# Three of 56 zero-fill pieces leave the Pool queue in parts of 4, 105, 13 and 6 rows

## The chip, the cores and the metric

The kernel runs on one core of one Trainium2 chip. A core has five instruction streams that matter here: TensorE (PE, with its weight loads as PEld), VectorE (DVE), ScalarE (ACT), GpSimd (POOL) and SyncE (SP), and sixteen DMA engines that move data between HBM and the on-chip memory. The metric is the device time of one execution in microseconds, and less is better. Times of whole runs are medians; durations inside a run come from one profiled execution.

## The reference

The reference computes a forward pass and its gradient for one token through four residual layers: attention (A), feed-forward (B), and the same A and B once more with the same weights.

```python
def _A_ref(x, k_cache, v_cache, wq, wo):
    W = min(4096, max(256, Sk // 4))                # 4096 of 32768 positions
    q = (x @ wq).reshape(B, Sq, Hq, Dh)             # 32 heads of 128
    k = jnp.repeat(k_cache[:, :, Sk - W:, :], rep, axis=1)
    v = jnp.repeat(v_cache[:, :, Sk - W:, :], rep, axis=1)
    p = softmax(q @ k * Dh ** -0.5)
    return (p @ v) @ wo
def _B_ref(x, w1, b1, w2):
    h = x @ w1 + b1
    return (h * tanh(softplus(h))) @ w2
x = x + _A_ref(_layernorm(x), ...); x = x + _B_ref(_layernorm(x), ...)   # twice
```

The outputs are x, and the gradients with respect to x, the two caches, wq, wo, w1, b1 and w2. The attention sees only the last 4096 of 32768 positions of each cache, so seven eighths of the two cache gradients, 56 MiB of bf16, are zeros and still have to be written.

## The kernel before, in words

All matrices are streamed from HBM in chunks of 128 rows by 4096 bf16 values (1 MiB, 8 KiB a row) through a ring of eight slots plus a few borrowed homes (`Ring`, issues at line 71 on the SP queue). A slot that is released lets the next load in the list start. The forward pass multiplies chunk by chunk, the backward pass turns chunks with TensorE (line 474) or takes row dots on VectorE (line 451). At the end the weight gradients are formed as outer products in PSUM (`unit_dw`, line 1051; `units_kv`, line 1086), copied out by `evac` to VectorE (line 306) or ScalarE (line 309), whichever a running cost count has as less loaded, and stored by `store` (lines 1025 and 1030) on the SP queue, in transfers of 512 KiB to 1 MiB. Before those outer products can start, row forms of the vectors are gathered with small transfers: `rowize` (line 1015), `rowize_f` (line 861), `take_back` (line 819) and `twins` (line 1043), all of them on SP.

The schedule is written by hand: each engine runs its instructions in program order, and the framework adds semaphore waits. Transfers of one queue take their completion semaphores from eight in turn, so an issue waits until the transfer that used that semaphore before is complete.

The zeros are 56 pieces of 128 rows by 4096 values. The list `zjobs` holds their destinations, `zt` is an on-chip tile of zeros, and `zeros(n, after)` issues the next n pieces on the Pool queue (line 265). With `after`, Pool first copies one element of a tile that the computation is about to write (line 260, into `pz`), so that the pieces are held back until that value exists. Calls of `zeros` are spread over the program from the second forward layer on. The ones of the last attention backward layer (`attn_bwd(0, ...)`) sit in its hooks: 2 pieces in `do1` at chunk 5, 4 in `dp1`, 4 in `dq1` once `DQC` is there, 2, 1 and 1 in `dn1` at t = 3, 6 and 7, and 2 after the layer. Counted from 0, `dq1` issues pieces 46 to 49.

Other instructions on Pool at that time are the copy at line 909 (before `dp1`'s pieces) and the one-element copies. On SP the loads are over by then; the small transfers of the list above and later the stores stand in its queue.

Of the kernel before, what the change touches and what calls it, by code (L numbers as in the profile page):

```python
# [15 lines left out]
P = 128  # L16
# [77 lines left out]
def kernel(  # L94
# [22 lines left out]
    nc = tc.nc  # L117
# [13 lines left out]
    def sb(shape, dtype, name):  # L131
        return keep.tile(shape, dtype, name=name)
# [24 lines left out]
    ZC = 4096  # L157
    zt = sb([P, ZC], BF16, "zt")
# [36 lines left out]
    for hi in range(4):  # L195
        r = slice(32 * hi, 32 * hi + 32)
# [9 lines left out]
    DQC = sb([P, HQ, 2], BF16, "DQC")  # L206
# [39 lines left out]
    zjobs = []  # L246
    for out_t in (out_2, out_3):
        for g in range(G):
            dst = out_t[0, g, 0:ZR, :].rearrange("(p r) d -> p (r d)", p=P).rearrange("p (r c) -> p r c", c=ZC)
# [7 lines left out]
    def zeros(n, after=None):  # L257

        if after is not None and zjobs:
            nc.gpsimd.tensor_copy(pz[0:1, pz_n[0] % 16:pz_n[0] % 16 + 1], after[0:1, 0:1])  # L260
            pz_n[0] += 1
        for _ in range(n):
            if zjobs:
                dst = zjobs.pop()
                nc.gpsimd.dma_start(dst, zt[:])  # L265


    KEEP_Q = (5, 6, 7)
# [519 lines left out]
    def last_da(k):  # L788

        for c in (5, 6):  # L790
            if k == 0:
                da_dots(c)
            else:
                ring.release(("2", 0, c))
        if k:
            nc.gpsimd.memset(zt[:], 0.0)
            zeros(1)

    def wo_hook1(c):
        if c == 0:  # L800
            zeros(7, OC[:, 0, 1:2])
        if c:
            conv(1)
# [18 lines left out]
    put_by("OC", OC, HQ)  # L822
    put_by("NA", NA, TD)
    zeros(8, x3)
    sB1 = mlp_fwd(1, x3, st3, lambda: conv(1, "A"))
    put_by("NB", NB, TD)
# [180 lines left out]
    def rowize(cols, n, base, off):  # L1007

        b = big().bitcast(BF16)
        nc.tensor.transpose(b[0:2 * n, 0:P], cols[:].rearrange("p n l -> p (n l)"), ident_bf[:])  # L1010
        k = rt_n[0]
        rt_n[0] += 1
        nc.scalar.copy(rt[0:2 * n, k, :], b[0:2 * n, 0:P])
        for l in range(2):
            nc.sync.dma_start(ROWS[base + l:base + l + 1, off:off + n * P].rearrange("o (t p) -> o t p", p=P),
                              rt[l:2 * n:2, k, :])
# [40 lines left out]
    def units_rows(base, nblk, out):  # L1057

        for c in range(nblk // 4):
            s = stage_free.popleft()  # L1060
            for tt in range(4):
                n = 0
                while n < 2:
                    m = unit_dw(base, NOFF + (4 * c + tt) * P, 512 * n, s[:, tt * D + n * 512:(tt + 1) * D], 2 - n)
                    n += m
                    store(out.rearrange("(c p k) d -> p c (k d)", p=P, k=4)[:, c], s, 2 * tt + n - m, 2 * tt + n, 8,
                          c == nblk // 4 - 1)
                    yield
# [110 lines left out]
    def dq1():  # L1179
        stage_free.extendleft(KT[:, g].rearrange("p t d -> p (t d)") for g in range(G))  # L1180
        todo[1].append(units_rows(32, HQ, out_5))
        rowize(DQC, HQ, 0, NOFF)
        zeros(4, DQC[:, 0, 0:1])

    def dn1(t):
        if t in (3, 6, 7):
# [8 lines left out]
    def units_a0(k):  # L1195
# [3 lines left out]
        work(4)  # L1199

    g0 = attn_bwd(0, sA0, g1, ("o", 3), ("q", 3), (), dict(do=do1, dp=dp1, dq=dq1, dn=dn1), units_a0)
    zeros(2, g0)
    g0b = sb([P, TD], BF16, "g0b")
# [49 lines left out]
```

## Time and profile before

| | |
|---|---|
| median of three timed runs | 450.8 us (450.39 to 451.2) |
| profiled execution | 450.36 us |
| its span | 448.6 us |
| bytes moved, mean rate | 181.40 MB, 404 GB/s |
| HBM read, written | 81.84 MB, 98.62 MB |
| zero pieces on queue 0 | 56 issues of 1024 KB, 20.5 us from issue to landing (median) |
| first and last issue of a zero piece | 114.7 and 334.7 us |
| queue 8 (instructions) | 44 packets of 16 KB |

The page's line of engines gives busy time, share of the span and number of instructions. The slices cut the span in 40 equal parts. In the table of stretches a line has the stretch, its length, the busy time of PE, PEld, DVE, ACT and POOL with their instruction counts, the granted TensorE clock, the busy share of the 16 DMA engines and the GB/s moved. The share is a sum of packet times over 16 engines and can pass 1 by a per cent, since the packets of an engine overlap a little. A wait line reads: engine, what it was about to do, what it waited for, microseconds in total, times, longest. A timeline line has start, length, engine, line and operation, how often, and in brackets the idle time before it with what ended it. Beside these views the trace has the time of each completion increment: a transfer over 16 engines has 16 of them.

### The profile page before, as it was taken

How to read it: one execution, taken by the hardware profiler on the slowest of the kernel's cores; microseconds unless marked ns; L12 is line 12 of the kernel's file. 1: busy time of each engine (PE TensorE's matmuls, PEld its weight loads, DVE VectorE, ACT ScalarE, POOL GpSimd, SP SyncE). 2: the span in 40 equal slices, each digit the busy share in tenths (PEclk: the TensorE clock that was granted, in tenths of full speed). 3: DMA queues.
4: the chain of work that ended last, by engine and by line, in shares of the span. 5: the costliest groups of instructions: out<-in, count | busy, mean ns of one | idle time of the engine just before them, and what ended most of it. 6: DMA issues, size and time to landing. Idle time of an engine off the chain costs nothing.

```text
span 448.6 us, 12825 instructions
## 1 busy us (share of the span) xinstructions
PE 313.9 (70%) x5681; PEld 239.7 (53%) x5681; DVE 261.2 (58%) x516; ACT 210.0 (47%) x242; POOL 38.9 (9%) x86
## 2 busy tenths in 40 slices
PE   3845542465699797986988666797966988899600
PEld 3735532455586686986986545787941222235300
DVE  4504746367551664864477447663566999998600
ACT  2501101011058576870474441570647999999600
POOL 1000000001222212102101001012130000000000
PEclk9955555556559899995798657986765555555555
DMA  8999999979999999999999999999999999999993
GB/s 336 420 420 418 421 420 418 418 312 427 393 421 422 422 420 415 398 420 423 424 423 422 427 423 419 424 393 422 424 406 415 400 417 419 417 421 408 377 408 143
DMA packets 28085, 181.40 MB, mean 404 GB/s; under 512 B 3674, under 2 KB 3702, under 8 KB 9590
## 3 DMA queue, kind: packets, MB, share of 16 engines
q1 hardware_dynamic: 19874, 121.84, 66.1%
q0 software_dynamic: 8064, 58.72, 31.5%
q8 instruction: 44, 0.72, 0.6%
q14 instruction: 11, 0.09, 0.1%
q10 hardware_dynamic: 92, 0.02, 0.0%
HBM read 81.84 MB, written 98.62 MB: 402 GB/s over the span
## 4 chain that ended last, share of the span: by engine, by line
DMA 53%; PE 22%; ACT 7%; DVE 7%; issue 4%; SPq 1%; ACTq 0%; DVEq 0%
DMA ring<-in_B_w_dram 13%; DMA W<-in_A_wo_dram 8%; PE BIG L474 8%; DMA ring<-in_A_wq_dram 7%; DMA ring<-in_A_wo_dram 5%; DMA W<-in_A_wq_dram 5%; ACT ring L309 4%; DMA out_dram<-W 4%; DMA W<-in_B_w_dram 4%; PE TP L493 3%; DMA W<-dr_AC 2%; DMA W<-in_A_k_cache_dram 2%; PE wide L1051 2%; DVE KT L306 2%; PE SC L347 2%
## 5 line engine op out<-in xcount | busy, mean ns | idle before, releaser
L309 ACT COPY ring<-BIG 128x1024 bf16<-128x1024 bf16 x52 | 51.5, 1014 | 49.3 <-PE BIG L474 45.0
L1051 PE MATMUL wide<-W 2*128 2x512 bf16 x232 | 51.7, 597 | 10.7 <-ACT ring L309 1.7
L474 PE MATMUL BIG<-ident_bf,ring 128*128 128x128 bf16 x672 | 54.3, 233 | 1.8 <-issue 1.0
L474 PEld LDWEIGHTS <-ring 128*128 128x128 bf16 x768 | 52.0, 108 | 3.4 <-issue 2.6
L451 DVE CUSTOM_DVE_ANT_0 junk<-ring,SC 128x1024 bf16<-128x1024 bf16 x32 | 38.9, 1215 | 11.6 <-DMA ring<-in_B_w_dram 11.2
L1051 PEld LDWEIGHTS <-W 2*128 2x128 bf16 x240 | 12.6, 102 | 48.1 <-issue 43.7
L493 PEld LDWEIGHTS <-ring 128*128 128x128 bf16 x864 | 29.9, 98 | 10.0 <-issue 5.8
L309 ACT CAST ring<-wide 128x1024 bf16<-128x1024 f32 x35 | 33.9, 1040 | 2.0 <-PE wide L1051 0.9
L265 POOL DMA_DIRECT2D out_dram<-zt x56 | 29.7, 534 | 50.3 <-DMA out_dram<-zt 49.3
L306 DVE CAST ring<-wide 128x1024 bf16<-128x1024 f32 (+1 forms) x29 | 32.3, 1145 | 2.5 <-PE wide L1102 1.2
L309 ACT COPY KT<-BIG 128x1024 bf16<-128x1024 bf16 x22 | 21.6, 1007 | 21.4 <-PE BIG L652 19.5
L451 DVE CUSTOM_DVE_ANT_0 junk<-ring,DSX 128x1024 bf16<-128x1024 bf16 x24 | 29.4, 1224 | 0.8
L306 DVE COPY ring<-BIG 128x1024 bf16<-128x1024 bf16 x32 | 21.8, 689 | 12.8 <-PE BIG L474 10.2
L474 PE MATMUL BIG<-ident_bf,W 128*128 128x128 bf16 x280 | 23.8, 235 | 3.4 <-DMA W<-in_A_wo_dram 2.5
L309 ACT COPY W<-BIG 128x1024 bf16<-128x1024 bf16 x20 | 20.0, 1015 | 10.0 <-PE BIG L474 9.8
L536 PE MATMUL MV<-NA,ring 128*128 128x1 bf16 x512 | 15.3, 165 | 13.2 <-DMA ring<-in_A_wq_dram 11.7
L536 PEld LDWEIGHTS <-ring 128*128 128x128 bf16 x512 | 14.7, 104 | 14.0 <-DMA ring<-in_A_wq_dram 12.5
L474 PEld LDWEIGHTS <-W 128*128 128x128 bf16 x288 | 19.3, 115 | 4.0 <-DMA W<-in_A_wo_dram 2.6
L1102 PE MATMUL wide<-W 32*128 32x256 bf16 x128 | 20.0, 403 | 0.9 <-ACT ring L309 0.6
L347 PE MATMUL YR<-ring,AC 128*32 128x256 bf16 x208 | 11.1, 372 | 11.7 <-DMA ring<-in_B_w_dram 9.3
L309 ACT CAST KT<-wide 128x1024 bf16<-128x1024 f32 x18 | 17.7, 1064 | 3.2 <-PE wide L1051 3.0
L306 DVE CAST KT<-wide 128x1024 bf16<-128x1024 f32 (+1 forms) x14 | 15.4, 1141 | 6.3 <-PE wide L1051 6.2
(272 smaller groups left out, 521.3 us busy)
## 6 DMA issues: line engine op xcount, KB each, us to landing
out_dram<-zt POOLq DMA_DIRECT2D x56, 1024.0 KB, 20.5
ring<-in_A_wq_dram SPq DMA_DIRECT2D x24, 1024.0 KB
ring<-in_A_wo_dram SPq DMA_DIRECT2D x14, 1024.0 KB
ring<-in_B_w_dram SPq DMA_DIRECT2D x13, 1024.0 KB
W<-in_A_wo_dram SPq DMA_DIRECT2D x10, 1024.0 KB
W<-in_B_w_dram SPq DMA_DIRECT2D x8, 896.0 KB
out_dram<-ring SPq DMA_DIRECT2D x13, 512.0 KB
out_dram<-ring SPq DMA_DIRECT2D x6, 1024.0 KB
```

Of the source, the lines that this page charges most:

```text
L265: nc.gpsimd.dma_start(dst, zt[:])
L306: nc.vector.tensor_copy(dst, src)
L309: nc.scalar.copy(dst, src)
L347: nc.tensor.matmul(bank[32 * j:32 * j + 32, 0:n].rearrange("p (g a) -> p g a", a=m.shape[-1]), lhsT=vec.to_broadcast([P, 32]), rhs=m, star ...
L451: nc.vector.tensor_tensor_reduce(out=out, in0=a, in1=vec, scale=1.0, scalar=acc if i else 0.0, op0=ALU.mult, op1=ALU.add, accum_out=acc)
L474: nc.tensor.transpose(b[:, i * P:(i + 1) * P], block(w, i) if block else w[:, i * P:(i + 1) * P], ident_bf[:])
L493: nc.tensor.matmul(out, lhsT=w[:, i * P:(i + 1) * P], rhs=rhs_of(i), start=fresh[0], stop=last and i == n - 1, skip_group_check=True)
L536: nc.tensor.matmul(q_ps[:, h:h + 1], lhsT=ch[:, h * P:(h + 1) * P], rhs=NA[:, t, l:l + 1], start=(k == 0 and h == 0), stop=(k == TD - 1), ...
L1051: nc.tensor.matmul(b[:, 512 * i:512 * i + 512], lhsT=R[at:at + 2, lo:lo + P], rhs=R[at:at + 2, ro + 512 * i:ro + 512 * i + 512], start=Tru ...
L1102: nc.tensor.matmul(b[:, k * 256:(k + 1) * 256], lhsT=RT[32 * g:32 * g + 32, a, tp, :], rhs=YS[32 * g:32 * g + 32, :], start=True, stop=Tru ...
```

## The change

In `dq1` the call for four pieces is replaced by one whole piece and three that are cut into parts. The new function `zeros_beside` issues, for each piece, three transfers of 4, 105 and 13 whole rows, and one for the last 6 rows in which the 8 KiB rows are seen as 16 blocks of 512 bytes, with the block index outermost on both sides. The bytes written are the same, and so is their source, a tile of zeros.

```diff
+    SPARED = 3
+
+    def zeros_beside(n):
+        for _ in range(n):
+            dst = zjobs.pop()
+            at = 0
+            for k in (SPARED + 1, 105, 16 - SPARED):
+                nc.gpsimd.dma_start(dst[at:at + k, :], zt[at:at + k, :])
+                at += k
+            r = P - at
+            nc.gpsimd.dma_start(dst[at:P, :].rearrange("a (b c) -> b a c", b=16),
+                                zt[0:16, 0:r * (ZC // 16)].rearrange("b (a c) -> b a c", a=r))
...
     def dq1():
...
         rowize(DQC, HQ, 0, NOFF)
-        zeros(4, DQC[:, 0, 0:1])
+        zeros(1, DQC[:, 0, 0:1])
+        zeros_beside(3)
```

On the Pool queue the four issues of line 265 after the copy of `DQC` become one issue of line 265 and twelve in the order 4, 105, 13, 16x6 blocks, three times over (lines 277 and 280 of the changed kernel). Each of the thirteen takes the next of the eight semaphores. No other engine's instructions change or move.

## The prediction

> **What bounds the kernel now.** I read the page's slices first, then the DMA queues, then a table of stretches, then the tail by itself, then the Pool engine's instructions, then the waits.
>
> ```profile
> PE 313.9 (70%) x5681; PEld 239.7 (53%) x5681; DVE 261.2 (58%) x516; ACT 210.0 (47%) x242; POOL 38.9 (9%) x86
> ...
> GB/s 336 420 420 418 421 420 418 418 312 427 393 421 422 422 420 415 398 420 423 424 423 422 427 423 419 424 393 422 424 406 415 400 417 419 417 421 408 377 408 143
> ...
> q1 hardware_dynamic: 19874, 121.84, 66.1%
> q0 software_dynamic: 8064, 58.72, 31.5%
> q8 instruction: 44, 0.72, 0.6%
> ```
>
> No compute engine passes 70%, while the transfers run at about 420 GB/s in nearly every slice: the kernel is bound by its 16 DMA engines. Queue 1 carries loads and results (issued by SP), queue 0 the zero pieces (issued by Pool), queue 8 the fetching of instructions.
>
> ```profile
> 340.00:352.00 12.00, 10.23 (x44) 2.26 (x44) 11.83 (x11) 11.98 (x14) 0.00 (x0) 0.50 1.01 412
> 352.00:354.00 2.00, 1.48 (x11) 0.46 (x10) 2.00 (x3) 1.84 (x4) 0.00 (x0) 0.50 0.87 342
> 354.00:418.00 64.00, 57.73 (x314) 21.15 (x315) 58.50 (x56) 61.03 (x66) 0.00 (x0) 0.50 1.01 416
> 418.00:422.00 4.00, 3.79 (x26) 2.11 (x21) 3.62 (x4) 3.82 (x5) 0.00 (x0) 0.50 0.81 326
> 422.00:441.00 19.00, 0.00 (x0) 0.00 (x0) 1.06 (x1) 0.30 (x1) 0.00 (x0) 0.50 1.01 403
> 441.00:447.50 6.50, 0.00 (x0) 0.00 (x0) 0.00 (x0) 0.00 (x0) 0.00 (x0) 0.50 0.07 28
> ```
>
> The last two columns are the DMA engines' busy share and GB/s. Compute is over by about 423; the rest is draining stores. From 441.0 the share is 0.07, one sixteenth. Finer, in 40 slices of 437 to 449 us:
>
> ```profile
> GB/s 396 437 410 437 382 410 369 437 382 437 437 423 314 55 55 41 27 27 27 27 27 27 27 27 27 27 14 27 27 27 27 27 27 27 0 0 0 0 0 0
> ```
>
> 27 GB/s is a sixteenth of 437. **One DMA engine works alone for 6.3 us, from 441.0 to 447.3, and the kernel ends with it.** The span is 448.6, the profiled execution 450.36, the median of the three timed runs 450.8.
>
> How that engine came to be late stands in the trace's semaphore records: each transfer of 128 rows has 16 landings, one for each engine's 8 rows. Some zero pieces, numbered from 0 (us):
>
> ```
> piece  issued  1st landing  15th    16th
>   #9   142.14    158.14    160.71  160.80
>  #22   174.66    193.52    198.77  203.86
>  #42   304.24    309.43    312.27  315.63
>  #43   304.77    311.97    314.78  319.12
>  #44   305.29    314.39    317.24  321.80
>  #45   305.82    316.84    319.68  324.60
>  #46   313.38    319.30    322.12  327.58
>  #49   314.94    326.68    329.61  335.55
> ```
>
> The 16th falls behind as the 16 KB instruction packets of queue 8 come by (44 of them, 0.88 to 1.1 us each, some 6.5 us apart while PE is busiest), which fits one engine carrying them all. Which one it is the trace doesn't number. But the two 7-row transfers of line 861 land 7 times, the last 7.5 us behind the sixth (312.48, 319.96), and the 2-row transfer of line 819 lands twice, 0.08 apart: the late engine serves a transfer of 7 rows and not one of 2. If small transfers take the engines from 0 on, it is one of 2 to 6; engine 3 fits.
>
> ```profile
> 313.38 2.10 POOL L265 DMA_DIRECT2D out_dram<-zt  x4
> 325.16 0.17 POOL L260 COPY pz<-dnp 1x1 f32<-1x1 f32 x1 [9.68 <-DVE dnp L451]
> ...
> POOL out_dram L265 <- DMA out_dram<-zt: 49.3, 21, 4.6
> ```
>
> The first line is the step that changes: four issues, 0.53 us each, without a wait. The last says why a fifth could wait: in 21 cases an issue of a zero piece came 0.28 us after the 16th landing of the piece eight before it. Pool has eight transfers in flight and no more.
>
> **The change: relief.** #46 stays whole; #47, #48, #49 become four transfers each. Dealt on around the 16 engines, 4 rows fall on engines 0 to 3, 105 = 15 x 7 on 4 to 15 and 0 to 2, 13 on 3 to 15, and the last 6 rows are cut in 16 for all. Engine 3 gets 2.375 rows instead of 8, each other 8.375. A piece takes 2.46 us (first landings 319.30 to 326.68, three pieces), 0.31 a row: engine 3 saves 3 x 5.625 x 0.31 = 5.2 us, the others get 3 x 0.375 x 0.31 = 0.35. Alone, that would end the late engine at 442.1 and the others at 441.4.
>
> **The change: the price.** Twelve transfers go through eight places, so four places now hold one piece, not four, and Pool must wait for landings on the late engine. By the table (+0.28): #46 and the parts of 4, 105, 13 rows go out at 313.38 to 314.95; the 6-row part waits for #42 (315.91); the second piece's parts for #43 (319.40), #44 (322.08), #45 (324.88), #46 (327.86); the third piece's 4 rows follow at 328.39, its 105 rows at 328.92 (before: all by 315.5). Meanwhile 15 engines run dry: the mean of the first 15 landings of #46 is 320.4, so the first cut piece is done at 323.0, and queue 1 has nothing to fill in with, since the last load's own 16 landings end at 316.9 and the first store is issued at 340.3.
>
> Let L be the time from an issue to the first packet when queue 0 is empty. Rows: 114.65 to 119.02 (4.4), 132.07 to 135.60 (3.5), 295.91 to 299.69 (3.8). In all three, queue 1 was busy, so some packets of 0.31 us came ahead; the idle engine's L lies lower, and its floor is the 1.3 us in which an 8-row transfer on a hardware queue, the first of the program, is issued and landed (0.73 to 2.03). [...] I take 3.2, the nearest row less one packet. [...]
>
> The third piece is then done on all engines at 328.92 + L + 7 rows and 1 row (2.46) + 6 blocks of 512 bytes (an estimate of 0.2, between 18 ns for a 256-byte packet and 47 to 56 for 1 KB) = 331.6 + L = 334.8. Before, the last of the 15 had #49 done at 329.61, the late one at 335.55. From here the work is the same: 441.0 - 329.61 = 111.4 us for the 15 (engines further ahead then ran dry at 352 and 418, in the table of stretches, so theirs is about that too), and 447.3 - 335.55 = 111.75 for the late one, which restarts with #50, issued at about 330.75, at 330.75 + 3.2 = 333.95. Ends: 446.2 and 445.7. So the relief of 5.2 and the 6.3 us lone tail are nearly eaten by a gap of some 6 us that the 15 engines did not have: **447.3 - 446.2 = 1.1, less 0.1 for nine more completion packets an engine (9 ns and a small gap each): 1.0 us gained.** In general 4.2 - L.
>
> Nine more issues cost Pool 9 x 0.53 = 4.8 us. The three one-element copies of line 260 and pieces #50 to #55 behind them slide from 325.2 to about 330.5; nothing but Pool's own issues waits for those copies, and #50 (330.75 + L) comes before the third piece is done. The small transfers of lines 819 and 1043 (11.05 and 7.30 us on the chain of waits) share engines with queue 0 and get faster when it is empty; stores may begin up to 4 us earlier. I count that at nothing: the DMA engines, not compute, set the end, and compute is done 18 us before 441. If that cover went, a late first store would show one to one.
>
> **The rivals.** *Every part starts at engine 0.* Then engine 3 gets 1 + 7 + 1 + 0.375 = 9.375 rows, 1.375 more than now: the late engine ends 3 x 1.375 x 0.31 = 1.3 us later. The 15 may run dry unharmed, being 6.3 us ahead. Result 452.1, slower by 0.3%. It decides as soon as the split does not carry on where the last part stopped. For it: SP's small transfers look as if they begin at the same engines each time. Against: the sizes 4, 15 x 7 and 13 sum to exactly two rounds of 16, which only makes sense for dealing on. [...] No run here shows which holds for these forms.
>
> *The engine named is not the late one, or the dealing begins elsewhere.* The late engine gets 0.375 rows a piece more and the extra completions: + 0.45, 451.2.
>
> *The gap does not open* (the waits are not on these places): relief in full, 447.3 to 442.1, 445.6. The 21 waits speak against it.
>
> [...]
>
> **How the numbers follow.** Forecast case 0.60: 450.8 - 1.0 = 449.8, own range (L from 1.7 to 5) 448.3 to 451.7; of it 0.36 faster, 0.20 same, 0.04 slower, 0.2% (0.9 us) being about what a measurement of this kernel can tell. All from engine 0: 0.25, 452.1 with 0.5 either way, 0.06 same, 0.19 slower. Wrong engine: 0.10, 0.06 same, 0.04 slower. No gap 0.03, faster. Something dearer, 0.02, slower. Sums: 0.39, 0.32, 0.29. The range takes both large cases: 448.2 to 452.4.
>
> **What would show it.** Right: Pool's issues of lines 277 and 280 at about 315.9, 319.4, 322.1, 324.9, 327.9, and 328.9 for the third 105 rows; the DMA share between 323 and 335 at about 0.5 to 0.6; no stretch of 27 GB/s at the end, the 16 engines stopping within 1 us; the second and third 105-row parts landing without waiting for the late engine. Wrong: a lone tail of 7 us or more (all from engine 0); a tail unchanged (wrong engine); a DMA share of 1.0 through 323 to 335 (no gap). It fails most easily on the dealing and on L.

## The result and the profile after

The changed kernel takes 457.7 us in the median (456.9 to 459.0) beside 450.9 of the kernel before, timed on the same chip: a ratio of 1.015, with an interval of 1.0133 to 1.0169. It is 6.9 us slower. The forecast was 449.8, its range ended at 452.4. The profiled execution, the longest of the four, took 458.99 us with a span of 457.2 (before: 450.36 and 448.6).

The page of the changed kernel, first the engines, then GB/s in the 40 slices of the span, then the three queues:

```profile
PE 315.0 (69%) x5681; PEld 240.6 (53%) x5681; DVE 261.5 (57%) x516; ACT 209.9 (46%) x242; POOL 43.5 (10%) x95
...
GB/s 331 423 418 420 420 421 418 417 313 421 392 421 418 419 414 410 399 419 421 422 420 424 424 412 368 421 423 422 257 225 411 412 417 418 417 421 413 407 408 214
...
q1 hardware_dynamic: 19874, 121.84, 65.2%
q0 software_dynamic: 8304, 58.72, 31.7%
q8 instruction: 44, 0.72, 0.6%
```

PE, DVE and ACT do the same work. POOL has nine issues more. The bytes are the same, in 240 packets more. What is new stands in slices 29 and 30: 257 and 225 GB/s where there were 424 and 406. Stretches of the same trace show that hole and the end (columns: stretch, length, busy time of PE, PEld, DVE, ACT and POOL, granted TensorE clock, DMA share, GB/s). First the hole before the change, then after it:

```profile
328.00:336.00 8.00, 5.32 (x70) 2.60 (x70) 4.39 (x15) 4.21 (x9) 2.64 (x7) 0.56 1.02 414
```

```profile
316.00:328.00 12.00, 11.49 (x223) 11.10 (x222) 7.37 (x12) 7.37 (x8) 2.74 (x6) 0.80 0.95 354
328.00:336.00 8.00, 3.22 (x107) 2.65 (x105) 4.91 (x12) 0.37 (x1) 2.29 (x5) 0.69 0.37 93
336.00:350.00 14.00, 10.04 (x44) 2.55 (x44) 8.47 (x12) 11.69 (x19) 4.08 (x11) 0.50 0.98 367
```

And the end of the changed kernel:

```profile
442.00:446.00 4.00, 0.00 (x0) 0.00 (x0) 0.00 (x0) 0.00 (x0) 0.00 (x0) 0.50 1.02 406
446.00:450.00 4.00, 0.00 (x0) 0.00 (x0) 0.00 (x0) 0.00 (x0) 0.00 (x0) 0.50 1.03 409
450.00:454.00 4.00, 0.00 (x0) 0.00 (x0) 0.00 (x0) 0.00 (x0) 0.00 (x0) 0.50 0.40 161
454.00:458.00 4.00, 0.00 (x0) 0.00 (x0) 0.00 (x0) 0.00 (x0) 0.00 (x0) 0.50 0.05 19
```

From 328 to 336 us six tenths of the DMA time are empty. At the end most engines work to about 451 (before: 441), and a few go on, the last of them to 456.0 (before: one, to 447.3). So the fifteen lost ten microseconds and the late one 8.7: the tail that was to be taken away is still there. That more than one engine is in it is in part no work of the change: in piece #42, before any part was issued, the 14th and 15th landings are already 3.2 and 4.0 us behind the eighth (before: 1.6 and 2.1). The Pool queue in its timeline (start, length, engine, line, operation, how often, idle time before and what ended it):

```profile
314.49 0.53 POOL L265 DMA_DIRECT2D out_dram<-zt  x1
315.02 1.57 POOL L277 DMA_DIRECT2D out_dram<-zt  x3
317.16 0.56 POOL L280 DMA_DIRECT2D out_dram<-zt  x1 [0.57 <-DMA out_dram<-zt]
320.73 0.51 POOL L277 DMA_DIRECT2D out_dram<-zt  x1 [3.01 <-DMA out_dram<-zt]
323.58 0.56 POOL L277 DMA_DIRECT2D out_dram<-zt  x1 [2.34 <-DMA out_dram<-zt]
326.50 0.52 POOL L277 DMA_DIRECT2D out_dram<-zt  x1 [2.36 <-DMA out_dram<-zt]
332.52 0.56 POOL L280 DMA_DIRECT2D out_dram<-zt  x1 [5.50 <-DMA out_dram<-zt]
```

The waits are where the prediction put them, 1.1 to 1.6 us later, up to the last one: 332.52 instead of 327.86. It waits for the late engine's landing of piece 46, at 332.24 instead of 327.58. The landings (us; last three of sixteen) show what that engine did:

```
               issued   14th    15th    16th
#45 whole      307.19  322.73  323.47  326.22
#46 whole      314.49  326.83  326.86  332.24    6.0 after #45; before: 3.0
#47   4 rows   315.02  327.03  327.06  332.44
    105 rows   315.52  329.67  331.26  334.49
     13 rows   316.06  329.86  331.66  334.68
    6x16 blk   317.16  330.07  331.87  335.07
#48 105 rows   323.58  332.23  333.89  337.00
#49 105 rows   334.77  340.99  343.73  343.91
#50 whole      336.51  344.28  346.94  347.46
```

**The last landing is 2.05 us later over the first 105-row part, as 7 rows take: the engine that was to be spared has rows in it.** From the last landing of #45 to that of #50 lie 21.2 us (before: 324.60 to 338.02, 13.4), for no more than 0.375 rows a piece more. Most 8 KB packets of queue 0 take 309 ns. Between 316 and 350 us 75 of 1146 took over 550 ns, a cluster of them some 600, twice the usual (before: 7 of 1365). In the four stretches of 6 us from 320 on their mean was 357, 409, 414 and 354 ns (before: 313 to 318). The trace doesn't say which engine moved a packet, so that the long ones are the late engine's is not shown.

Two sums from the packet records are used below. *Dry*: the part of 16 engines' time without a packet between 316 and 350 us, as us an engine (0.0 before, 6.1 after). *Stretched*: what the 8 KB packets of queue 0 took over 309 ns in the same stretch, divided by 16 (0.5 before, 2.8 after). Smaller packets, into which some of the experiments cut rows, are not in it.

### The profile page after: what moved, and what is told of

Same layout as the page of the kernel before. It is cut to its first block, busy times and chain, and to the rows that moved or that the text cites. A ratio compares the mean times of both kernels' runs of the same rounds, so it can differ in the third digit from the quotient of the medians.

```text
span 457.2 us, 12834 instructions
## 1 busy us (share of the span) xinstructions
PE 315.0 (69%) x5681; PEld 240.6 (53%) x5681; DVE 261.5 (57%) x516; ACT 209.9 (46%) x242; POOL 43.5 (10%) x95
## 4 chain that ended last, share of the span: by engine, by line
DMA 34%; PE 33%; ACT 10%; DVE 9%; issue 5%; ACTq 1%; SPq 0%; DVEq 0%
DMA ring<-in_B_w_dram 13%; PE BIG L490 9%; DMA W<-in_A_wo_dram 7%; DMA ring<-in_A_wq_dram 6%; ACT ring L325 6%; DMA W<-in_B_w_dram 4%; PE TP L509 3%; PE BIG L668 3%; DMA W<-in_A_k_cache_dram 2%; PE wide L1067 2%; ACT KT L325 2%; DMA W<-W 2%; PE wide L1118 2%; PE YR L363 2%; DVE W L322 2%
## 5 line engine op out<-in xcount | busy, mean ns | idle before, releaser
L490 PEld LDWEIGHTS <-ring 128*128 128x128 bf16 x768 | 51.5, 107 | 3.2 <-issue 2.4
L467 DVE CUSTOM_DVE_ANT_0 junk<-ring,SC 128x1024 bf16<-128x1024 bf16 x32 | 38.9, 1215 | 9.5 <-DMA ring<-in_B_w_dram 9.0
L509 PEld LDWEIGHTS <-ring 128*128 128x128 bf16 x864 | 29.5, 97 | 11.1 <-issue 5.8
L265 POOL DMA_DIRECT2D out_dram<-zt x53 | 28.2, 535 | 42.1 <-DMA out_dram<-zt 41.1
L552 PEld LDWEIGHTS <-ring 128*128 128x128 bf16 x512 | 14.6, 103 | 13.3 <-DMA ring<-in_A_wq_dram 11.9
L325 ACT CAST VS<-wide 128x1024 bf16<-128x1024 f32 x18 | 18.0, 1039 | 0.7 <-PE wide L1067 0.4
```

What stands on the lines that cost most here:

```text
L325: nc.scalar.copy(dst, src)
L467: nc.vector.tensor_tensor_reduce(out=out, in0=a, in1=vec, scale=1.0, scalar=acc if i else 0.0, op0=ALU.mult, op1=ALU.add, accum_out=acc)
L490: nc.tensor.transpose(b[:, i * P:(i + 1) * P], block(w, i) if block else w[:, i * P:(i + 1) * P], ident_bf[:])
L509: nc.tensor.matmul(out, lhsT=w[:, i * P:(i + 1) * P], rhs=rhs_of(i), start=fresh[0], stop=last and i == n - 1, skip_group_check=True)
L552: nc.tensor.matmul(q_ps[:, h:h + 1], lhsT=ch[:, h * P:(h + 1) * P], rhs=NA[:, t, l:l + 1], start=(k == 0 and h == 0), stop=(k == TD - 1), ...
```

## The experiments

The first theory after the result, a guess that the runs were to test: rows read from neighbouring partitions share a way out of the on-chip memory (the "ports" of the expectations), and a part's few rows lie in neighbouring partitions; the engine named is the wrong one; the dry stretch does the rest. The rivals: completions or issues as such, or one of the three alone.

**Parts alone.** A kernel that leaves all the computation out and only issues zero transfers from Pool, one kind at a time, with and without neighbouring source partitions.

> This kernel computes nothing of the layers: it only issues zero transfers on the Pool queue in a quiet chip, each shape by itself, with four fills of about 3.5 us between them, and two large copies on SP at the end. Theory P (ports): rows read from neighbouring partitions share a way out of the on-chip memory, so 4 rows from partitions 0 to 3 need 4 x 0.31 = 1.24 us where 4 rows taken from every ninth partition need 0.31; the same for 13 rows (1.24 against 0.31) and, less, for 105 rows (2.5 to 2.8 against 2.2). Theory L (eight places alone): no difference between neighbouring and spread partitions, landings within 0.2 us of each other. On the dealing: if it carries on around the engines, four transfers of 4 rows back to back put one row on each of 16 engines and the fourth lands about as soon as the first; if every one starts at engine 0, the fourth lands about 0.9 us after the first. Beside a large copy of 4 rows on SP, which keeps four engines busy, the first of two 4-row transfers is late and the second not if the dealing carries on from engine 0; both are late if each starts there.

From issue to last landing: 128 rows 4.2 us; 4 rows 2.7 from neighbouring partitions and 1.8 from partitions 9 apart; 13 rows 2.7 and 1.9; 105 rows 4.5 and 3.9; the sixteen blocks 2.1. The first packet starts 1.1 us after the issue, and engines without a row land 1.41 us after it. So L of the prediction is 1.1 and not 3.2; in the hole of the changed kernel it is 1.2 (issue 332.52, first packet 333.72). Four rows from partitions 0 to 3 take 4 x 0.31 as if there were one path for the four: each of their packets took 0.98 us in the mean, those from partitions 9 apart 0.31. Whether there is such a path no record says. The 0.31 us a row in the prediction held for whole pieces, where this price isn't seen (317 ns a packet). The change's own four parts of one piece, issued one behind the other, had 442 ns a packet and took 7.2 us from the first issue to the last landing (184.30 to 191.54).

That row of four parts also bears on the dealing. In the 4 rows twelve engines land by 185.81 and the four that have a row at 187.06 or later; in the 105 rows behind them the engine without rows lands at 186.64. So it is none of those four. Dealt on round the engines, it would be the fourth of them: the 105 plain rows were not dealt on.

**Sources apart.** The changed kernel, with source rows 9 partitions apart; the 105 rows read 15 partitions seven times each, and the sixteen blocks partitions 7 apart.

```diff
-                nc.gpsimd.dma_start(dst[at:at + k, :], zt[at:at + k, :])
+                if k == 105:
+                    nc.gpsimd.dma_start(dst[at:at + k, :].rearrange("(j s) c -> j s c", s=7),
+                                        zt[0:127:9, None, :].to_broadcast([15, 7, ZC]))
+                else:
+                    nc.gpsimd.dma_start(dst[at:at + k, :], zt[0:9 * k - 8:9, :])
...
-                                zt[0:16, 0:r * (ZC // 16)].rearrange("b (a c) -> b a c", a=r))
+                                zt[0:106:7, 0:r * (ZC // 16)].rearrange("b (a c) -> b a c", a=r))
```

> The changed kernel with the same rows written by the same transfers in the same order; only the on-chip rows that the zeros are read from differ: every ninth partition for the 4, 13 and 105 rows (each of the 15 shares of 7 rows reads one partition seven times), every seventh for the 16 blocks. Theory P: packets of 600 us-thousandths and more between 320 and 345 us vanish, and the time returns to what the prediction had, 449 to 452 us. Theory L: the issues wait as before, the gap stays, 456 us or more.

453.65 us, ratio 1.0060 (1.0045 to 1.0075): 4.1 us less than the changed kernel, and between the two theories' 449 to 452 and 456 or more. Stretched falls from 2.8 to 1.6 us, dry stays (6.7). The late engine still lands 2.5 us after its landing before in the 105-row part.

**Eight places alone.** Each of the three pieces in four quarters of all 128 rows (1024 columns each).

> The same three pieces leave as four transfers of 128 rows by 1024 values each: twelve transfers through the eight places as in the change, but all 16 engines dealt alike and every row read where it was before. Theory L: the gap opens as in the changed kernel and the time is 455 us or more. Theory P: the 15 engines lose some 5 us that they had to spare, the late engine does not run dry, 450 to 452 us.

451.0, ratio 1.000 (0.999 to 1.0009). The waits come at 317.3 to 330.9 as in the change, dry is 3.4 us, and nothing is lost: the fifteen have that much to spare before the late engine ends.

**Which engine.** Four small transfers of 3, 4, 5 and 6 rows on the SP queue, beside everything else; first after `rowize_f`, then earlier.

> The kernel before with four tiny SP transfers of 3, 4, 5 and 6 rows beside those of line 861. If small SP transfers take the engines from 0 on and the late engine is engine 3, the last landing of the 4-, 5- and 6-row transfers is about 7 us behind the others and that of the 3-row transfer is not. If it is another engine, the first late one is the transfer of 3 (engine 2), 5 (engine 4) or 6 rows (engine 5), or none (engine 6). The time should stay within 2 us of the kernel before.

They went out at 317.9 to 320.4, and none landed late: no answer. By 321.63 the late engine was done with what SP had issued before, and all landings of the four come behind that, at 322.63 to 326.25.

```diff
+            for k in (3, 4, 5, 6):
+                nc.sync.dma_start(dram.tile([k, P], BF16, name=f"probe{k}")[:], zt[0:k, 0:P])
             rowize(GB, TD, 96, 0)
```

> As the run before with four tiny SP transfers of 3, 4, 5 and 6 rows, which were issued when the late engine's SP ring was empty; now they go out right behind the last loads, near 297 us, where the 8-row transfers of line 1015 show one landing 7 us behind. If the late engine is engine 3, the transfers of 4, 5 and 6 rows have one such landing and that of 3 rows has none.

Issued at 297.4 to 306.5. Of the 3 and 4 rows all land by 309.37 and 309.99. Of the 5 rows four land by 310.65 and the fifth at 318.96, of the 6 rows five by 312.48 and one at 319.38. **The late engine is the fifth that a small transfer takes, engine 4 if they count from 0, not engine 3.** This takes it that each of the four begins at the same engine. The landings agree (none late of 3 and of 4 rows, one of 5 and one of 6); that this first engine is the one numbered 0 is the author's way of counting.

**How Pool deals.** A kernel without the computation again, with shares of known weight one behind the other. A share is what one engine gets of a transfer.

> Computes nothing of the layers; zero transfers on a quiet chip whose shares are 4 to 16 rows an engine, so that it shows in the landings which engines a transfer uses. [...] If the dealing carries on around the engines: four 4-row transfers of 8 rows a share land within 2.5 + 1.6 us of the first issue; after one of them, the next 4-row transfer beside a copy on SP's first four engines is not delayed; the sequence 4, 15, 13 shares (of 8, 7 and 4 rows) ends with loads of 15, 12 and 11 rows on 3, 1 and 12 engines; 15 shares beside SP's four engines have three delayed. If each starts at engine 0: the four end after 10 us; the 4-row transfers beside SP's four engines are all delayed; the sequence ends with 19, 11, 7 and 0 rows on 4, 9, 2 and 1 engines; four of 15 are delayed.

Four transfers of 4 shares each, in a form whose source has a repeated dimension (each share reads one partition several times): 12 engines without rows in the first, 8 idle ones in the second, 4 in the third, none in the fourth. In this form the dealing carried on round the engines; four transfers of plain rows in a row were not in this run. All four read the same four partitions, and their engines took up to 10 us for 8 rows of 0.31.

**The fifth engine instead of the fourth.** Parts of 5, 105, 12 and 6 rows, with sources apart and with neighbours.

```diff
-    SPARED = 3
+    SPARED = 4
```

> The cut of the changed kernel with parts of 5, 105, 12 and 6 rows, so that by the dealing round the engines the fifth engine (engine 4) is the one with 2.375 rows a piece, and with sources 7 or 9 partitions apart. Theory (engine 4 is late, ports cost 4.1 us, the rest of the loss is that the engine spared was another): relief of 5.2 us in full, the gap by the eight places still open, time from issue to landing 1.4 us as measured alone: 450.9 - 4.2 + 1.4 = 448.1, within 447.0 to 449.5; the 105-row parts then land on 15 engines within about 1 us, none 5 us late. Rival (the late engine is not engine 4, or the dealing begins elsewhere): as with parts of 4, 105 and 13, about 453.7, with one landing of every 105-row part some 6 us behind.

> Only the number of the engine is changed (parts of 5, 105, 12 and 6 rows), sources are neighbouring partitions as in the changed kernel. Theory: the ports still cost 4.1 us beside the kernel with spread sources, so 448.1 + 4.1 = 452.2, within 450.5 to 454, and 5.5 us less than the changed kernel. If the late engine were not relieved: 457.7 as the changed kernel. If ports were not the reason of the difference between the two sources: as the kernel with spread sources, 448.

453.85 (ratio 1.0075, 1.0051 to 1.0099; the profiled execution 456.6) and 456.5 (1.012, 1.0105 to 1.0135). The theory's 448.1 and 452.2 failed: the 105-row parts still end with a lone landing 2.2 us behind its last, 7 rows. Either the engine or the dealing was still misread.

**Three pieces together.** Fewer transfers: 5 rows of pieces 46 to 48, then 120 rows of each as 15 shares with one row behind it, then 2 rows of all.

> A version meant to be better: the same three pieces less one number (46, 47 and 48) leave in eight transfers instead of twelve: 5 rows of all three, then for each piece 120 rows as 15 shares of 8 and one row for the engine that is next, then the last 2 rows of all three; sources 9 partitions apart; piece 49 whole behind them. By the dealing engine 4 gets 6 rows of the three pieces instead of 24, no other over 27, and only four large transfers wait behind the landings on the late engine. Theory: the late engine ends 18 x 0.31 = 5.6 us earlier, at 441.7, the others 0.4 to 0.9 later than 441.0, no gap over 1 us: 450.9 - 5.4 = 445.5, within 444.5 to 447. Rival (engine 4 is not the late one): the late engine gets 24 to 27 rows, 451 to 452.

453.5 (1.0046 to 1.0073), far from the 445.5 of the theory. The late engine lands 0.20 us after its last landing in the first 120 rows, so it is spared there, but 2.6 and 3.5 us after in the second and third: the single rows did not move the dealing on as assumed.

**Place by place.** Pieces 42 to 54 in two transfers of j and 16-j shares, a share reading one partition eight times.

> The kernel before, with pieces 42 to 54 each cut into two transfers: j shares of 8 rows and 16-j shares of 8 rows, j = 2 for piece 42, 3 for 43, ... 14 for 54 (sources 7 partitions apart, so that a share reads one partition). Every engine still gets 8 rows of each piece. The late engine's landing of the part in which it has its 8 rows comes about 2.5 us after its landing before that, of the other part 0.2 us after. So the j from which the first part holds the late engine's rows gives its place in the dealing of the Pool queue. Theory until now (place 4, counted from 0): first part from j = 5 on, second part for j = 2, 3, 4. Rival (the dealing of this queue starts at another engine than that of SP's small transfers, and the late engine stands at place 14, as the landings of the run with three pieces together suggest, where the 120 rows of the first piece are the only ones that it is spared): the second part for every j from 2 to 14. Time: near 451, up to 3 us more by waits on the eight places.

518.3 us in a single execution. The mean 8 KB packet took 607 to 873 ns in the stretches of 10 us between 310 and 350, the longest 4.5 us, and no landing could be read. What this shows is a price; the kernel has many shares in flight that read the same few partitions.

Then pieces 40 to 55 in two plain parts, the first 120 rows and the last 8.

> The kernel before, with pieces 40 to 55 each cut into a transfer of the first 120 rows (15 shares of 8) and one of the last 8 rows (8 shares of one), all with neighbouring source partitions as in a whole piece. A piece has 23 shares, so the dealing moves on by 7 engines a piece, and the one engine without rows in the 120 is, piece after piece from 40, at place 15, 6, 13, 4, 11, 2, 9, 0, 7, 14, 5, 12, 3, 10, 1, 8. The late engine's landing of a 120-row part comes about 2.5 us after its landing before (8 rows), and about 0.2 us after it in the one piece in which it has none; that piece gives its place. Theory of the engine numbered 4 in both queues: piece 43. Rival from the run with three pieces together: place 14, piece 49. If the dealing starts each transfer at the same engine, the late engine is spared in all of them or in none. Time: 451 to 455, by port sharing of the 8-row parts (up to 0.9 us a piece alone, mostly beside other packets) and the eight places.

458.3, a single execution. In every one of the sixteen 120-row parts one engine lands ahead, in all but the first three some 2.5 us after the issue, while the others come 2 to 14 us behind it, and in none does the late engine have a pause:

```
                issued    1st     2nd   ...   16th
#42  120 rows   305.07  308.12  311.46      317.68
#43  120 rows   306.09  308.55  313.92      321.04
#44  120 rows   307.65  310.10  316.40      324.00
#45  120 rows   312.48  315.03  318.85      327.22
#46  120 rows   317.97  320.46  322.97      330.68
```

An engine that is idle in one piece and loaded in the next can't keep ahead like that: it is the same engine each time. **The transfers of 120 plain rows left out the same engine in all sixteen pieces; only the forms with a repeated dimension carried on.** So 105 plain rows are read here as 15 shares of seven on the same engines each time; if they begin at engine 0 these are engines 0 to 14, and the one spared is engine 15. That start is the author's estimate, and for 4 and 13 plain rows it is taken over, not shown. The prediction weighed a fixed start against dealing on, and took the one that these transfers do not follow.

**All parts in the form that carries on.** The split of the change with 5, 105, 12 and 6 rows, the 5 and 12 rows cut in halves of 4 KB from a repeated source. This is what the prediction took the change to do, with the right engine. Against the kernel with 5, 105, 12 and 6 rows and sources apart:

```diff
-                    nc.gpsimd.dma_start(dst[at:at + k, :], zt[0:9 * k - 8:9, :])
+                    nc.gpsimd.dma_start(dst[at:at + k, :].rearrange("j (h c) -> j h c", h=2),
+                                        zt[0:9 * k - 8:9, None, 0:ZC // 2].to_broadcast([k, 2, ZC // 2]))
```

> The split of the change (three pieces in four parts each), with 5, 105, 12 and 6 rows, all in the form that carries on round the engines (the single rows are cut in two halves of 4 KB with a repeated source dimension), sources 7 or 9 partitions apart. This is what the prediction took the change to do, with the right engine. Theory: the engine that is late has no landing 2.2 us behind its last in a 105-row part; relief of 5.6 rows a piece or 5.2 us; a gap by the eight places remains: 448.1, within 447 to 450. If the gap by the eight places is dearer than the relief: 451 to 453, with the 16 engines stopping within 2 us of each other. If the dealing is still not understood: 453.7 as the last two with spread sources, and the late engine 2.2 us or more behind in the 105-row parts.

The late engine now lands 0.20 and 0.19 us after its landings before in the 105-row parts of the first two pieces (331.21 and 331.41; 332.18 and 332.37): it has no rows there, the dealing is settled. The time is 453.05 all the same (ratio 1.0051, 1.0033 to 1.0069), by the second of the theories: the hole is as deep as in the changed kernel, dry 6.7 us, and the engines stop nearly together at 448 to 450.

```profile
328.00:336.00 8.00, 4.36 (x58) 1.95 (x55) 4.68 (x15) 3.20 (x7) 5.05 (x12) 0.61 0.43 149
```

**Relief without more issues.** Fewer transfers than the twelve: in one kernel 5 shares of one row, 15 shares of 21 and 12 of 4 in the last group of pieces; in another pieces 46 to 48 as 5 shares of 3 rows, 120 rows three times from their own partitions, and 12 shares.

> A version meant to be better, by the reading of the walk of places: transfers of plain rows are dealt from engine 0 each time, the late engine is the fifth, and only forms with a repeated source dimension (15 shares of 7, of 8) carry on round the engines. The last 896 zero rows (pieces 49 to 55) leave as 5 shares of one row, 15 shares of 21 rows, 12 shares of 4 rows, all in the form that carries on, then 4 x 128 and 16 rows in the plain form. The fifth engine gets 1 + 4 + 33 = 38 rows instead of 56, engines 0 to 3 get 55, the others 58. Only 5 issues stand in the place of 4, so no wait on the places beyond those of before. Theory: the late engine ends 18 x 0.31 = 5.6 us earlier (441.7 of a span, from 447.3), the others 0.6 later (441.6): 450.9 - 5.4 = 445.5, within 444.3 to 447. The landings of the 15 shares of 21 rows: one early, 15 about 6.5 us after those before, and the early one is the engine that was behind. If the late engine is another, or the form does not carry on: 451.5 or more, with a lone engine at the end.

> A version meant to be better: pieces 46 to 48 leave as 5 shares of 3 rows, 15 shares of 24 rows (120 rows of all three pieces, each row's partition read three times, in the partition order of a whole piece) and 12 shares of 6 KB for the last 3 rows of each piece; 49 whole behind them. Four issues as before, so no wait on the places beyond those of before; all three in the form that carries on round the engines. The fifth engine gets 3.75 rows of the three pieces instead of 24, engines 0 to 3 get 27, the others 24.75. Theory: the late engine ends 20.25 x 0.31 = 6.3 us earlier (441.0), the others at 441.2 to 441.9: 450.8 - 5.4 = 445.4, within 444 to 448. If the order of the engines after so long a transfer sets off more port sharing, as the run with one long transfer suggests: 449 to 454 with all engines stopping within 3 us. If the form does not carry on: 450 to 452 with the lone engine at the end as before.

The first: no hole (dry 0.3 us), but the twelve timed executions lie between 449.2 and 455.7, median 453.4 (ratio 1.0039, 1.0008 to 1.0069), not at the 445.5 of the theory. In its profile (an execution of 450.7) the late engine has no rows in the 15 shares, and by the order of the landings another takes 12.0 us for its 21 rows (326.25 to 338.24), 0.57 a row, and is the late one from there on. The second: 457.7 (1.0133 to 1.0176). The last landing of the 120 rows is 9.5 us behind the one before, so the late engine was not spared; a repeated dimension alone doesn't make this form carry on.

**One piece instead of three.**

> The changed kernel with one of the three pieces cut instead of all: pieces 46 to 48 whole, 49 in parts of 4, 105, 13 and 6 rows, neighbouring sources as in the changed kernel. Seven issues in the place of four, so only the last three wait (about 316, 319 and 322 us), with three whole pieces queued ahead of them. Theory (most of the loss is that the engines run dry behind the waits on the late engine's landings, and the rest grows with the number of cut pieces): no dry stretch between 316 and 350 (under 0.5 us an engine, against 6.1 in the changed kernel), and 450.9 + 0.4 to 0.8 for ports and the late engine's 0.4 rows = 451.5, within 450.7 to 452.3. Rival (the loss is by the parts themselves, ports and completions, and goes with their number): a third of 6.9 us, 453.2.

452.9 (1.0024 to 1.0052): 1.9 us, more than my bound and near the rival's third of the loss. No hole behind the waits (dry 1.6 us, most of it at 344 to 348, where the first store is issued at 346.5 instead of 340.3); stretched 2.3 us from one cut piece.

**The same parts, spread in time.** One cut piece at the end of each of three groups (pieces 41, 45 and 49), so that whole pieces lie ahead of every wait. First with the change's own parts.

```diff
-            zeros(2, do1_acc[:, 4 * c:4 * c + 1])
+            zeros(1, do1_acc[:, 4 * c:4 * c + 1])
+            zeros_beside(1)
...
-        zeros(4)
+        zeros(3)
+        zeros_beside(1)
...
-        zeros(1, DQC[:, 0, 0:1])
-        zeros_beside(3)
+        zeros(3, DQC[:, 0, 0:1])
+        zeros_beside(1)
```

> The changed kernel's own three cut pieces (parts of 4, 105, 13 and 6 rows, neighbouring sources), but one at the end of each of the groups of 2, 4 and 4 pieces before the copy of DQC's step and in it (pieces 41, 45 and 49), so that whole pieces lie queued ahead of every wait. Same parts, same bytes, other places. Theory (the dry stretch behind the waits on the late engine's landings is the largest part of the loss, 6.1 of some 10 us by which the 15 engines end later): idle time from 316 to 350 under 1.5 us an engine, 15 engines stop by 446, and 452.3, within 451 to 454. Rival (the parts themselves): 456 to 458 as the changed kernel.

457.3 (1.0115 to 1.0163), as the changed kernel. The hole is gone:

```profile
328.00:336.00 8.00, 5.02 (x157) 4.42 (x155) 5.86 (x13) 1.19 (x2) 2.06 (x6) 0.77 0.98 311
```

Dry is 0.6 us, the fifteen engines stop at about 447 instead of 451, and the late one still ends at 453. **My theory of the dry stretch fell: without relief it costs nothing, because the late engine sets the end.** The parts themselves cost the time, as the rival had it: stretched is 3.8 us here.

Then the form that carries on, with engine 4 spared, and the same with engine 3 spared (4, 105, 13 and 6), nothing else changed.

> The same places in time with parts of 5, 105, 12 and 6 rows in the form that carries on, sources 7 or 9 partitions apart: relief of the fifth engine (16.9 rows, 5.2 us) without the dry stretch. The prediction's case of no gap. Theory: late engine 447.3 - 5.2 = 442.1, others 441.4 plus stretched packets of about 1.5 us: 450.8 - 3.5 = 447.3, within 445.5 to 450. Rival (relief at that point of time is given back: the first store or the small transfers come later, or packets are stretched more): 450.5 to 453 with idle time between 340 and 360.

> The last kernel with one number changed: parts of 4, 105, 13 and 6 rows instead of 5, 105, 12 and 6, in the same form that carries on, at the same places in time. By the dealing the fourth engine (engine 3) is spared and the fifth keeps 8.375 rows a piece. Theory (engine 4 is the late one, and its relief is worth up to 5.2 us where nothing runs dry): the profiled execution has a lone engine at the end again, some 5 us, and 452 to 453 beside the 447.7 of the profiled execution of the last; the median of the timed runs 2 to 5 us above the 451.1 of the last. Rival (the low times of the last were chance in the order of packets, not relief): the same spread and median as the last, 450 to 452, and no lone engine in the profile.

Engine 4: median 451.1, ratio 0.9989 (0.9961 to 1.0017), but its twelve executions lie between 447.5 and 455.9; the profiled one took 447.7. So the profiled execution is where the theory put it (447.3) and the median where the rival did (450.5 to 453). Engine 3: 457.2 (1.0133 to 1.016), between 456.4 and 458.3, the profiled one 456.4, more above the last kernel than the 2 to 5 us expected. The ends, first with engine 4, then with engine 3 spared:

```profile
438.00:442.00 4.00, 0.00 (x0) 0.00 (x0) 0.00 (x0) 0.00 (x0) 0.00 (x0) 0.50 0.96 383
442.00:446.00 4.00, 0.00 (x0) 0.00 (x0) 0.00 (x0) 0.00 (x0) 0.00 (x0) 0.50 0.10 42
```

```profile
442.00:446.00 4.00, 0.00 (x0) 0.00 (x0) 0.00 (x0) 0.00 (x0) 0.00 (x0) 0.50 1.02 408
446.00:450.00 4.00, 0.00 (x0) 0.00 (x0) 0.00 (x0) 0.00 (x0) 0.00 (x0) 0.50 0.32 128
450.00:454.00 4.00, 0.00 (x0) 0.00 (x0) 0.00 (x0) 0.00 (x0) 0.00 (x0) 0.50 0.05 22
```

With engine 4 spared all engines stop between 441 and 444.5; with engine 3 spared one works alone from about 449 to 453.5. One number in the split is worth 6.0 us of the median.

Side by side (rows of the late engine in the three pieces that are cut, by the dealing found; before: 24):

| kernel | rows | dry | stretched | time |
|---|---|---|---|---|
| before | 24 | 0.0 | 0.5 | 450.9 |
| changed | 25.1 | 6.1 | 2.8 | 457.7 |
| quarters | 24 | 3.4 | 0.7 | 451.0 |
| sources apart | 25.1 | 6.7 | 1.6 | 453.65 |
| carries on, engine 4, together | 7.1 | 6.7 | 1.6 | 453.05 |
| change's parts, spread in time | 25.1 | 0.6 | 3.8 | 457.3 |
| carries on, engine 3, spread | 25.1 | 1.3 | 2.9 | 457.2 |
| carries on, engine 4, spread | 7.1 | 0.1 | 1.8 | 451.1 |

## Why the prediction was wrong

**Relief: the step failed twice.** "Engine 3 fits" was a guess among 2 to 6; it is engine 4 (the probes of 5 and 6 rows, and the pair with engine 4 or 3 spared). And "dealt on around the 16 engines" was not so for plain rows: no run shows them dealt on, and in 16 of 16 parts of 120 rows the same engine had none. If each part begins at engine 0, the change spares one that is not late (engine 15), and the late engine gets 0 + 7 + 1 + 0.375 = 8.375 rows a piece instead of the 2.375 of the forecast. Its landings in the 105-row part, 2.05 us behind its last, show the 7. The two rivals that said so were both right in part: dealing from engine 0 (chance 0.25) for the dealing, the wrong engine (0.10) for the load, + 0.375 a piece. That "the sizes 4, 15 x 7 and 13 sum to exactly two rounds of 16" was an argument from what the change was meant for, not from the trace.

**The price of a row: mis-sized, and the largest error.** 0.31 us a row holds in whole pieces. From #45 to #50 the late engine took 21.2 us where it took 13.4 before, so the wrong-engine rival's + 0.45 was in truth + 6.9. That parts cost more than their rows by themselves is shown: 442 ns a packet alone on the chip, 4.1 us between the two sources in the whole kernel, and the whole loss still there without the hole. Why is argued: packets of twice 309 ns, and four neighbouring rows at 0.98 us a packet where four rows apart take 0.31, fit a way out of the on-chip memory that neighbouring rows share. That is the author's reading: no record names such a way, and why whole pieces (313 to 318 ns in the mean, beside 354 to 414 with parts) would be free of its price is not shown. How the loss divides among the parts stays open: with sources apart it is 2.8 us when the parts stand together and engine 3 is spared, but 6.2 in the form that carries on, spread in time, and no run here explains that pair.

**The gap: the mechanism was right, its place in the sum was not.** Pool waits for the late engine's landings through eight places, the hole is there, and at 6.1 us an engine it is the size forecast ("some 6 us"), in part by luck: the last wait ended 4.7 us later than forecast, and L was 2 us shorter. But it was to set the end, at 446.2, because the late engine was thought relieved. Not relieved, the late engine sets the end, and the hole costs nothing (quarters 0, spread in time 0.4 of 6.9). With the relief it does cost: 453.05 with the parts together, 451.1 spread. L was 1.1 to 1.2, not 3.2 and under the prediction's floor of 1.3; no run shows an L of 5. Put right, this term alone would have raised the forecast gain to some 3 us.

**Nine issues, 4.8 us of Pool: right.** Pool is busy 43.5 us instead of 38.9. The copies behind slid further than forecast, to 336.4 instead of 330.5, by the last wait. **The stores "counted at nothing":** they did not begin up to 4 us earlier but 3.1 us later, the first at 343.45 (before: 340.31). In the changed kernel that left nothing dry, since queue 0 had zero pieces to move until 366. With one piece cut it did: there queue 0's last piece lands on thirteen of the engines from 345.15 to 347.63, the first store goes out at 346.45, and 1.6 us are dry. The 18 us that compute has to spare at the end did not cover a late first store.

**What would show it** was well chosen: "a lone tail of 7 us or more (all from engine 0); a tail unchanged (wrong engine)". The tail of some 5 us with a few engines in it fits the second.

What stays open: why the kernel with engine 4 spared and no hole spreads from 447.5 to 455.9 us over twelve executions, where the kernel before spreads over 1. Its profile shows what is to be had, 3 us, but as a median it is no better than the kernel before. Why engine 4 is the late one, by the instruction packets as the prediction had it, rests on their coming together in time; no run moved them. Which partitions an engine reads in a whole piece no run shows, and no split that keeps to them was tried.

## What to carry to other kernels

Before work is moved off one DMA engine, measure which engine is late and how the queue deals that very form of transfer: a few probes of 3, 4, 5 and 6 rows and a row of parts gave both, and one engine beside the mark cost 6 us. The price of a row in transfers over all 128 partitions (317 ns a packet alone on the chip) was not that of the change's parts (442 ns); price parts from parts, alone and beside other traffic. The idle stretch in the middle cost 0 to 0.4 us where the engines that idled were not the last to end, and some 2 us where they were (453.05 beside 451.1).

## What was not expected of the hardware

- Transfers of 120 plain rows on the Pool queue left the same engine out each time (16 of 16), while forms of 4 or 15 shares with a repeated source dimension carried on round the engines: four of 4 shares left 12, 8, 4 and 0 engines idle, and behind 5 shares two parts of 15 shares spared the late engine (landings 0.20 and 0.19 us after its last).
- On the idle Pool queue the first packet started 1.1 us after the issue, an engine without rows posted its landing 1.41 us after it, and the last of 16 with 8 rows each 4.2 us after it.
- 8 KB packets that mostly took 309 ns in whole pieces took some 600 in a cluster when parts were in flight (75 of 1146 over 550 ns), 0.98 us in the mean where four rows were read from four neighbouring partitions, and 607 to 873 ns in the mean where many shares read a few partitions.
- With engine 4 relieved another engine took the late one's part in the run with 15 shares of 21 rows: 21 rows in 12.0 us, beside 6.5 at 0.31 a row.
